# Attention and SwiGLU FFN on one core: loads ordered by need, masks built on chip, four tiles ahead of the FFN, and q and k transposed by DMA

## The chip, the cores and the metric

The kernel runs on one core of one Trainium2 chip. The metric is the device time of one execution in microseconds (us). A profiled execution also gives a span, from the first to the last instruction, which stands about 2 us below the time. A program can also fall into a slower state with a lower granted TensorE clock.

## The reference, cut to what matters

```python
# q, k, v: (8 batches, 8 heads, 576 rows, 64), fp32
rel    = pos[:, None] - pos[None, :]
mask   = (rel >= 0) & (rel < 128)                   # causal window of 128
scores = (q @ k^T) / 8 - slope[h] * |rel|           # ALiBi; -1e9 outside the mask
x      = softmax(scores) @ v                        # -> (4608 tokens, 512)
g      = x @ w_gate                                 # 512 -> 1536
out    = (silu(g) * (x @ w_val)) @ w_out            # 1536 -> 512, fp32
```

## The kernel before

Two batches are taken together and cut into nine tiles of 128 rows; the fifth holds the last 64 rows of both. With four such pairs there are 36 tiles of q, k and v, called ranks here. The attention takes the tiles of a pair in the order of their rows, with the combined one last, and the scores of a tile need its own rank and the next: tile 4 of the attention needs ranks 5 and 6, and tile 9, the first of the second pair, ranks 9 and 10. The attention of a tile is: transpose q and k, scores, exp on ScalarE, product with a mask of ALiBi weights on VectorE, values, division, transpose of x. The FFN takes 512 tokens (four tiles) as a block. Its matmuls are mixed with the attention of later tiles in program order, and TensorE executes in that order.

Transposes of q and k run on TensorE, and VectorE copies them out of PSUM, the memory into which the program's matmuls write:

```python
pt = ps_a.tile([P, 8, P], FP16, name="pt", tag="a")
for j in range(4):
    nc.tensor.transpose(pt[:, j, :], tk[:, 2 * j:2 * j + 2, :], idm)
for j in range(4):
    nc.tensor.transpose(pt[:, 4 + j, :], tq[:, 2 * j:2 * j + 2, :], idm)
nc.vector.tensor_copy(kTs[s][:, :, cols], pt[:, 0:4, :])
nc.vector.tensor_copy(qTs[s][:, :, cols], pt[:, 4:8, :])
```

The attention emits the scores of tile i + 1 ahead of the values of tile i, always. Loads of the inputs and weights go through GpSimd's queue and convert fp32 to fp16 on the way. Their order at the start is:

```python
loads_to(1); load_w(wg2, wg_sb, 0, 128);   load_w(wv2, wv_sb, 0, 128)
loads_to(3); load_w(wg2, wg_sb, 128, 512); load_w(wv2, wv_sb, 128, 512)
loads_to(4); load_mask("lo")
# ... [cut: w_gate and w_val from column 512 on]
loads_to(5)
# ... [cut: w_out, two transfers]
loads_to(7); load_mask("hi"); load_mask("com")
```

The softmax here doesn't subtract the row's maximum and nothing guards it: scores larger than these inputs give would overflow.

## Time and profile before

| | before |
|---|---|
| time, median of 3 runs | 411.18 us (411.11 to 411.3) |
| span of the profiled run | 409.1 us |
| first gate matmul of the FFN | 59.3 us |
| long stage, from there to the last output matmul | 344.9 us, TensorE idle 3.6 |
| tail | 4.9 us |

The kernel is two stages: a start in which TensorE waits for loads, and a long stage in which TensorE is full. The prediction below shows the lines for that. In the profiles PE is TensorE, PEld its loads of weights, DVE VectorE, ACT ScalarE, POOL GpSimd and SP SyncE; L with a number is a line of the kernel. The DMA queues (packets, MB, and the sum of the packets' times as a share of 16 engines' span) and the time from issue to landing (columns: transfer, queue, kind and count, KB each, median us):

```profile
q0 software_dynamic: 118304, 18.88, 62.0%
q1 hardware_dynamic: 5968, 11.31, 8.1%
...
out_dram<-osb SPq DMA_DIRECT2D x32, 256.0 KB, 2.0
kn<-in_k_dram POOLq DMA_DIRECT2D x32, 128.0 KB, 3.7
```

The packet times of the converting loads (q0, 18.88 MB) add up to 62%. Packets overlap (the same kind of sum, the DMA share of the windows below, goes up to 2.43 here), so this tells how much is in flight, not how long the engines are busy. The hardware queue (q1: masks and output stores) has little to do, and an output store is in DRAM 2.0 us after its issue.

### The profile page before, as it was taken

How to read it: one execution, taken by the hardware profiler on the slowest of the kernel's cores; microseconds unless marked ns; L12 is line 12 of the kernel's file. 1: busy time of each engine (PE TensorE's matmuls, PEld its weight loads, DVE VectorE, ACT ScalarE, POOL GpSimd, SP SyncE). 2: the span in 40 equal slices, each digit the busy share in tenths (PEclk: the TensorE clock that was granted, in tenths of full speed). 3: DMA queues.
4: the chain of work that ended last, by engine and by line, in shares of the span. 5: the costliest groups of instructions: out<-in, count | busy, mean ns of one | idle time of the engine just before them, and what ended most of it. 6: DMA issues, size and time to landing. Idle time of an engine off the chain costs nothing.

```text
span 409.1 us, 6645 instructions
## 1 busy us (share of the span) xinstructions
PE 364.4 (89%) x2592; PEld 181.0 (44%) x2592; DVE 245.9 (60%) x500; ACT 173.8 (42%) x317; POOL 112.0 (27%) x170
## 2 busy tenths in 40 slices
PE   0571289999999999999999999999999999999995
PEld 0240134455545445444454454455544445444442
DVE  0351057876587567675885586758865864572550
ACT  1241055534455455445644555455444543323321
POOL 7974485053424211542260104111000000000000
PEclk9999999999999999999999999999999999999998
DMA  9999999269969652799696527654011000101104
GB/s 221 164 192 193 182 155 95 14 42 80 124 66 66 64 79 38 52 82 116 64 68 63 79 38 48 82 79 29 0 53 51 2 27 26 51 2 51 54 12 91
DMA packets 124304, 30.62 MB, mean 75 GB/s; under 512 B 114544, under 2 KB 119152, under 8 KB 124272
## 3 DMA queue, kind: packets, MB, share of 16 engines
q0 software_dynamic: 118304, 18.88, 62.0%
q1 hardware_dynamic: 5968, 11.31, 8.1%
q8 instruction: 20, 0.33, 0.3%
q14 instruction: 12, 0.10, 0.1%
HBM read 39.62 MB, written 9.44 MB: 120 GB/s over the span
## 4 chain that ended last, share of the span: by engine, by line
PE 73%; DMA 10%; DVE 7%; ACT 5%; issue 2%; POOL 1%; DVEq 0%; POOLq 0%; ACTq 0%
PE po L322 22%; PE pv L308 20%; PE pg L295 20%; DMA kn<-in_k_dram 6%; DMA wv_sb<-in_moe_w_val_dram 4%; ACT exr L223 4%; PE ps L209 3%; PE av L254 3%; PE px L281 3%; DVE uu L300 2%; PE pt L162 1%; PE pt L164 1%; DVE hT L310 1%; DVE exl L227 1%; DVE ex L227 1%
## 5 line engine op out<-in xcount | busy, mean ns | idle before, releaser
L308 PE MATMUL pv<-xT,wv_sb 128*128 128x512 f16 x432 | 112.0, 380 | 1.4 <-DVE uu L300 1.2
L295 PE MATMUL pg<-xT,wg_sb 128*128 128x512 f16 x432 | 112.0, 381 | 0.3
L300 DVE SCALAR_TENSOR_TENSOR uu<-tt,pg 128x512 f16<-128x512 f16 x108 | 73.8, 684 | 61.6 <-ACT tt L298 61.2
L322 PE MATMUL po<-wo_sb,hT 128*128 128x512 f16 x432 | 104.8, 379 | 0.9 <-ACT osb L326 0.7
L298 ACT ACTIVATE tt<-pg 128x512 f16<-128x512 f32 x108 | 65.1, 603 | 79.5 <-PE pg L295 77.6
L223 ACT ACTIVATE exr<-ps 128x512 f16<-128x512 f32 x128 | 67.4, 608 | 39.7 <-PE ps L209 39.7
L310 DVE TENSOR_TENSOR hT<-uu,pv 128x512 f16<-128x512 f16 x108 | 74.0, 685 | 8.3 <-PE ps L209 1.0
L143 POOL DMA_DIRECT2D kn<-in_k_dram x40 | 34.0, 853 | 113.3 <-PE pt L164 101.9
L308 PEld LDWEIGHTS <-wv_sb 128*128 128x128 f16 x432 | 40.8, 98 | 47.4 <-issue 4.4
L322 PEld LDWEIGHTS <-hT 128*128 128x128 f16 x432 | 40.0, 98 | 43.7 <-issue 3.9
L295 PEld LDWEIGHTS <-wg_sb 128*128 128x128 f16 x432 | 39.9, 98 | 43.8 <-issue 3.2
L227 DVE TENSOR_TENSOR ex<-exr,m_reg 128x1024 f16<-128x1024 f16 x48 | 33.1, 689 | 36.2 <-ACT exr L223 36.2
L326 ACT ACTIVATE osb<-po 128x512 f32<-128x512 f32 x36 | 21.6, 600 | 59.0 <-PE po L322 58.9
L282 ACT COPY xT<-px 128x512 f16<-128x512 f16 x36 | 21.0, 584 | 50.9 <-PE px L281 50.8
L162 PE MATMUL pt<-idm,kn 128*128 128x128 f16 x144 | 15.7, 238 | 27.9 <-DMA kn<-in_k_dram 27.0
L143 POOL DMA_DIRECT2D va<-in_v_dram x40 | 33.8, 851 | 7.3 <-POOL va L140 5.0
L143 POOL DMA_DIRECT2D qn<-in_q_dram x40 | 34.1, 854 | 5.1 <-DMA wo_sb<-in_moe_w_out_dram 2.9
L165 DVE COPY kT<-pt 128x512 f16<-128x512 f16 x36 | 15.1, 418 | 31.6 <-PE pt L164 31.4
L257 DVE TENSOR_TENSOR x<-av,rec 128x256 f16<-128x256 f32 x72 | 29.0, 419 | 0.7
L209 PE MATMUL ps<-qT,kT 64*128 64x256 f16 (+1 forms) x288 | 27.2, 282 | 2.3 <-DVE qT L166 2.3
L162 PEld LDWEIGHTS <-kn 128*128 128x128 f16 x144 | 11.1, 105 | 35.4 <-DMA kn<-in_k_dram 29.1
L281 PE MATMUL px<-idm,x 128*128 128x128 f16 x144 | 18.8, 230 | 5.5 <-DVE x L257 5.4
(27 smaller groups left out, 173.5 us busy)
## 6 DMA issues: line engine op xcount, KB each, us to landing
out_dram<-osb SPq DMA_DIRECT2D x32, 256.0 KB, 2.0
kn<-in_k_dram POOLq DMA_DIRECT2D x32, 128.0 KB, 3.7
qn<-in_q_dram POOLq DMA_DIRECT2D x32, 128.0 KB, 5.0
va<-in_v_dram POOLq DMA_DIRECT2D x32, 128.0 KB, 5.3
wo_sb<-in_moe_w_out_dram POOLq DMA_DIRECT2D x2, 768.0 KB, 16.4
wg_sb<-in_moe_w_gate_dram POOLq DMA_DIRECT2D x2, 512.0 KB, 8.7
wv_sb<-in_moe_w_val_dram POOLq DMA_DIRECT2D x2, 512.0 KB, 10.1
out_dram<-osb SPq DMA_DIRECT2D x8, 128.0 KB, 2.3
```

The lines of the kernel that those rows point to most:

```text
L143: nc.gpsimd.dma_start(t_[p0:p1, :, 0:D], src[b, :, r0:r0 + p1 - p0, :].rearrange("h p d -> p h d"))
L162: nc.tensor.transpose(pt[:, j, :], tk[:, 2 * j:2 * j + 2, :], idm)
L209: nc.tensor.matmul(two[par][:, j, o:o + w], kT[rows, pair, kcols], qT[rows, pair, cols], start=(j == 0 and n == 0), stop=(j == 1 and n == ...
L223: nc.scalar.activation(er[:, o:o + 2, :], banks[q4][par], AF.Exp, scale=scale)
L227: nc.vector.tensor_mul(e[:, o, :], er[:, o, :], m[:, o, :])
L281: nc.tensor.transpose(pt[:, kb, :], x[:, kb * P:(kb + 1) * P], idm)
L295: nc.tensor.matmul(pg, wg_sb[:, kb, ms], xT[n][:, kb, :], start=(kb == 0), stop=(kb == NKB - 1))
L298: nc.scalar.activation(tt, pg, AF.Tanh, scale=0.5)
L300: nc.vector.scalar_tensor_tensor(out=uu, in0=tt, scalar=1.0, in1=pg, op0=ALU.add, op1=ALU.mult)
L308: nc.tensor.matmul(pv, wv_sb[:, kb, ms], xT[n][:, kb, :], start=(kb == 0), stop=(kb == NKB - 1))
L310: nc.vector.tensor_mul(hT[n][:, m, :], uu, pv)
L322: nc.tensor.matmul(po, hT[n][:, m, j * P:(j + 1) * P], wo_sb[:, m, :], start=(m == 0), stop=(m == NMB - 1))
```

## The change

It has four intents: (1) load only one of the four masks and build the others from it on VectorE; (2) order the loads at the start by need; (3) let the FFN begin after four tiles, with the scores of tile 4 no longer ahead of the values of tile 3; (4) from rank 9 on, transpose q and k by DMA on SP's queue, which takes 216 transposes from TensorE and 54 copies from VectorE. The diff, cut to its core:

```diff
-QK_BY_DMA = False
+QK_DMA_FROM = 9
...
-    for name, m in (("reg", reg), ("lo", lo), ("hi", hi), ("com", com)):   # 4 masks, each loaded
+    nc.sync.dma_start(reg, reg_d.ap())                                     # 1 mask load
+    def make_lo():
+        nc.vector.memset(lo[:, :, 192:256], 0.0)
+        nc.vector.tensor_copy(lo[:, :, 0:192], reg[:, :, 0:192])
...                                                    [make_hi, make_com alike]
-        if QK_BY_DMA:
+        if rank >= QK_DMA_FROM:
+            for t_, dst in ((natk.pop(rank), kTs[s]), (natq.pop(rank), qTs[s])):
                 nc.sync.dma_start_transpose(
                     dst[:, :, cols], t_.rearrange("p h d -> p (h d)"))
...
-            if i < last:
+            if i < last and i != FIRST - 1:            # FIRST = 4
                 transposes_to(need_rank[i + 1])
                 after = scores(i + 1)
...
-            loads_to(i + 8)
+            if i >= FIRST:
+                loads_to(i + 7)
+                ahead(i)                               # DMA transposes, up to 4 tiles ahead
...
+            if i == FIRST - 1:
+                transposes_to(need_rank[i + 1])
+                for fs in scores(i + 1):
+                    ...
-    loads_to(1) ... loads_to(7)                        [the old order, above]
+    load_qk(0, "kq")
+    for r in range(4):
+        load_qk(r + 1, "q"); load_v(r); load_qk(r + 1, "k")
+    load_w(0, 128); load_w(128, 512)
+    load(5); load_v(4); load_w(512, 1024)
+    load(6); load_w(1024, 1536); load(7); load(8)
+    [then w_out]
...
-        target = base + step * (4.55 * 8) / per_block
+            blk, target = 0, base + 2 * max(0, step - 8)                    # block 0
+            target = base + 32 + (step - 24) * RATE * 8 / 36                # RATE = 5.2
```

Beside these: the tile of v has its column of ones written once instead of for every rank, the intermediate of the FFN lies in 18 column tiles instead of two whole blocks, and the combined tile has another order of slots. The transposes that stay on TensorE take one PSUM slot for q and one for k, and stand right before the scores that need them, no longer a tile ahead.

## The prediction

> **What bounds the kernel now.** I read the engine row and the 40 slices of the page first. TensorE is the busiest engine, but its row is full only from the seventh slice on:
>
> ```profile
> PE 364.4 (89%) x2592; PEld 181.0 (44%) x2592; DVE 245.9 (60%) x500; ACT 173.8 (42%) x317; POOL 112.0 (27%) x170
> ...
> PE   0571289999999999999999999999999999999995
> ...
> DMA  9999999269969652799696527654011000101104
> ```
>
> A slice is 10.2 us, so there are two stages. Up to about 59 us TensorE mostly waits while the DMA engines are full. After that TensorE is full and the DMA engines have room. The table of windows puts the cut where the first gate matmul starts (59.3) and where the last output matmul ends (404.2):
>
> ```profile
> 50.00:59.30 9.30, 7.44 (x65) 4.12 (x64) 4.48 (x14) 3.73 (x8) 9.12 (x19) 1.00 2.43 155
> 59.30:404.20 344.90, 341.27 (x2409) 167.93 (x2408) 229.97 (x458) 158.93 (x290) 69.38 (x100) 1.00 0.53 56
> 404.20:409.10 4.90, 0.00 (x0) 0.00 (x0) 0.00 (x0) 0.60 (x1) 0.00 (x0) 0.75 0.32 71
> ```
>
> The first number is the length, then the busy time of PE, PEld, DVE, ACT and POOL, the clock, the DMA share and GB/s. In the long stage TensorE idles for only 344.9 - 341.3 = 3.6 us: there only less TensorE work makes the kernel shorter. VectorE has 115 us free there. The tail is 4.9 us.
>
> The timeline of the first 60 us says what the first stage waits for:
>
> ```profile
> 9.35 0.61 PE L162 MATMUL pt<-idm,kn 128*128 128x128 f16 x4 [9.35 <-DMA kn<-in_k_dram]
> ...
> 14.54 1.04 PE L209 MATMUL ps<-qT,kT 64*128 64x256 f16 x8 [0.84 <-DVE qT L166]
> ...
> 38.89 0.61 PE L162 MATMUL pt<-idm,kn 128*128 128x128 f16 x4 [7.86 <-DMA kn<-in_k_dram]
> ...
> 49.03 0.61 PE L162 MATMUL pt<-idm,kn 128*128 128x128 f16 x4 [8.69 <-DMA kn<-in_k_dram]
> ```
>
> Three long waits, all for k tiles: the first tile (9.35), and ranks 5 and 6 (38.89, 49.03). A rank is one of the 36 tiles of 128 rows of q, k and v. Rank 6 is needed because the program emits the scores of tile 4 ahead of the values of tile 3, and the FFN needs tiles 0 to 3. In the issue order ranks 5 and 6 stand behind all of w_gate and w_val, and rank 6 behind w_out too.
>
> **What the Trainium skill says.** (1) "DMA: Bandwidth & Descriptors", section "Issuing engines are not separate DMA queues": transfers of all issuers run on the same 16 engines and interleave. The trace agrees: in the first 10 us the SP queue moved 1.87 MB (four masks, identity) and the GpSimd queue 0.35 MB; in the next 10, alone, the latter moved 1.62. (2) The same page, section "SWDGE vs HWDGE vs iDMA": casts go through GpSimd, transposes through SP or ACT. So the fp32 loads must stay on GpSimd, and the new transposes share SP with the output stores. (3) "VectorE: DVE Perf Modes", section "The three transpose paths": a 128x128 16-bit transpose is 390 ns on TensorE and 1309 ns through the DMA crossbar. The trace has 238 ns for one on TensorE, far less in a stream (below); no run here shows a DMA transpose yet. (4) "Advanced Engine Details and Errata", section "X-Bar Transpose (TRN2)", expects 350-400 GB/s for such DMAs. Sections (3) and (4) disagree about the new operation by an order of magnitude, which sets my range.
>
> **The change part by part.**
>
> *Start: masks.* Three of four masks are no longer loaded: 0.5 + 0.5 + 0.25 MB, 1.3 MB. At the 1.87 + 0.35 MB that moved between about 1.7 and 10 us (some 270 GB/s; the middle of that window ran at 300 to 390) this is about 4 us. The first k tile should land at 9.35 - 4 = 5.3 us. Building the masks takes VectorE eight instructions, estimated at 2 us in all from the 0.69 us of a 128x1024 product; by the instruction order they stand among the first copies, in idle time. GpSimd also loses 36 memsets of 0.165 us, which cost nothing.
>
> *Start: order of loads.* 0.131 MB at 155 GB/s is 0.85 us per tile, and the 0.85 us of GpSimd's own issue agrees. The order is k0 q0 q1 v0 k1 q2 v1 k2 q3 v2 k3 q4 v3 k4. From 5.3 that puts k1 near 8.9, k2 11.5, k3 14.1, k4 16.7. Then the first weight columns (0.26 MB at 200 GB/s) land near 18 and the next ones near 22.
>
> *Start: the chain.* With data there, compute sets the pace. In the old trace scores of tiles 0 to 3 start at 14.54, 19.15, 23.80 and 29.16: about 5.4 us a tile at the end, exp to mask to value to division to transpose, and none of the last ones waits for a DMA. The new k1 lands at 8.9, scores 0 start some 1.4 later (as 13.08 to 14.54 before), scores 1 at 13.1 (PSUM slots come free after the exps), then +4.65 and +5.36: scores 3 at 23.1, against 29.16. Tile 4's scores no longer stand ahead. In the old trace the products of tile 3 end at 33.08; values, division, transposes and copies add about 3.2, so 36.3, minus the 6.05 shift: the first gate matmul near 30.5. That is 29 us earlier than 59.3.
>
> *Long stage: transposes.* Back to back they cost TensorE less than their latency:
>
> ```profile
> 204.67 0.39 PE L162 MATMUL pt<-idm,kn 128*128 128x128 f16 x4
> 204.90 0.39 PE L164 MATMUL pt<-idm,qn 128*128 128x128 f16 x4
> 205.12 0.39 PE L162 MATMUL pt<-idm,kn 128*128 128x128 f16 x4
> 205.34 0.39 PE L164 MATMUL pt<-idm,qn 128*128 128x128 f16 x4
> 205.57 1.03 PE L308 MATMUL pv<-xT,wv_sb 128*128 128x512 f16 x4
> ```
>
> From start to start four take 0.22 us, so a rank (eight) takes 0.44, not 8 x 0.238. Before, 112 of the 144 k transposes fall after 59.3, so 28 ranks. After, only ranks 5 to 8 do. 24 ranks x 0.444 = 10.6 us leave TensorE. Added: the scores of tile 4 (0.6). The stage is 344.9 - 10.6 + 0.6 = 334.9. VectorE loses 54 copies of about 0.416, 22.5 us, from an engine that is not the bound.
>
> *DMA transposes.* 54 of 128 KB. Their loads have slack: GpSimd waited 101.9 us for TensorE to free k tiles. The new rate of 5.2 gives 8/1.156 = 6.9 FFN steps per tile, at 0.863 us plus 1.3 of attention: 7.3 us per tile, for two transposes. Output stores of 256 KB land in 2.0 us on SP's queue; with 2 to 2.5 us per transpose the pair takes about 5 and is hidden.
>
> *Losses.* After step 8 of block 0 attention runs at two steps per FFN step, one tile per 5.2 us, equal to the 5.4 us chain, and VectorE has about as much work there as TensorE (21 us each by count of instructions): I add 2.5 us. Scores 9, the first to need DMA transposes, come at about 62; k and q of ranks 9 and 10 come behind w_out and land from 52 to 56, and four transposes follow: I add 2 us.
>
> *Sum.* 30.5 + 334.9 + 2.5 + 2 + 4.9 = 374.8 of span. The time stands 2.1 above the span (411.2 against 409.1): 377.
>
> The per-column FFN tiles (18 buffers in place of two whole blocks), fewer memsets and the combined tile's changed slots cost the same number of main instructions; I give them nothing.
>
> **The rivals.**
> (a) *The DMA transposes become the pace.* With 4 blocks x 1.309 us one takes 5.2, a pair 10.5, against 7.3 available. From 53 us, 27 x 10.5 ends at 337; then about 3 for the last tiles, two FFN blocks (62), the last projections (10.4) and the tail: about 418, slower than now. TensorE executes in order, so late transposes stop the FFN too, and stores behind them on SP hold ScalarE. For it: the skill's smaller figure, and SP's order, which has up to 18 transposes between stores. Against it: section (4), and 16 engines that should work on the four blocks together.
> (b) *The start is won and given back.* The DMA engines are full to 60 us before; after, they must carry the same minus 1.3 MB. If the FFN begins at 30, block 0 could wait for weight columns or ranks 7 to 10 instead. By my landing times columns 512 on arrive at 31 (needed 37), rank 8 at 43 (needed 46): it fits narrowly. If it fails by 5 to 10 us: 382 to 387.
> (c) *The start is bound by the chain more than I think*, since each transpose group now takes its own PSUM slot (two per rank, of four that turn over): one more us a tile gives about 381.
> (d) *Everything hides*: no added losses, 372.
>
> **Range and chances.** The centre is the sum, 377. (d) and a start at 28 give 368; (b) and (c) together give about 390. Range 366 to 391. "Faster" fails only if (a) holds in nearly full size, since the start alone is worth 29 us: faster 0.92, same 0.04, slower 0.04.
>
> **What would show it.** The first k transposes at 5 to 6 us and the first gate matmul at 28 to 33 show the start. In the long stage: 216 fewer TensorE transposes, 54 fewer VectorE copies, stage length about 335 to 340 with idle below 10 us. (a) would show as TensorE waits for DMA before scores, throughout, and landings over 3.6 us; (b) as DMA waits between 30 and 65 us only. I am wrong if the gate matmul starts after 40, or if scores wait for transposes past the second batch pair.

## More of the kernel before

The outputs leave through three buffers and the queue of SP (SyncE), which does little else:

```python
opool = ctx.enter_context(tc.tile_pool(name="op", bufs=3))
# ...
osb = opool.tile([P, DM], FP32, name="osb", tag="osb")
nc.scalar.mul(osb, po, 0.5)                      # ScalarE, from PSUM
for p0, p1, r0 in rows_of(n, j):
    nc.sync.dma_start(out[r0:r0 + p1 - p0, :], osb[p0:p1, :])
```

## The result, and the profile after

| | before | after |
|---|---|---|
| time, median of 4 runs each | 411.14 us | 388.99 us (388.19 to 389.99) |
| span of the profiled run | 409.1 | 386.4 |
| first gate matmul | 59.3 | 29.8 |
| long stage | 344.9 | 351.8 |
| tail | 4.9 | 4.9 |

The long stage is counted to 4.9 us before the end in every run below; in the changed kernel the last matmul ends 0.4 us after that.

The ratio of the times is 0.9466, with a 95% interval of 0.9435 to 0.9497. A ratio here is the mean time of one kernel's fast runs over that of the other's of the same rounds, so it isn't quite the ratio of the medians. The result is correct. The kernel is faster, by 22 us where 34 were predicted, and the 388.99 lies near the upper end of the range.

First the engine row, the slices and the queues of the page after:

```profile
PE 356.6 (92%) x2376; PEld 169.8 (44%) x2376; DVE 232.8 (60%) x461; ACT 173.3 (45%) x317; POOL 108.8 (28%) x134
...
PE   2889996799999959999999999999999999999995
...
PEclk9999999699999978999999999999999999999999
DMA  9999999999999999999201020110011001002004
...
q0 software_dynamic: 118304, 18.88, 75.4%
q1 hardware_dynamic: 34912, 17.08, 23.3%
```

TensorE has 216 instructions fewer, as intended. Counting slices of 9.7 us from 0, its row is full from slice 3 on, but has two dents: slices 6 and 7 (58 to 77 us) and slice 14 (from 135 us). Under each dent, or just after it, the granted clock falls. The DMA row is new too: it is full through slice 18, up to some 180 us, where it had been loose from 70 us on. The times of the same 118304 load packets now add up to 75.4% instead of 62.0% of a longer span, and the hardware queue has 28944 packets more.

The windows (length, busy time of PE, PEld, DVE, ACT and POOL with the number of instructions, clock, DMA share, GB/s), the last for the whole long stage:

```profile
29.70:60.00 30.30, 29.34 (x204) 13.37 (x204) 23.11 (x47) 15.48 (x30) 18.18 (x22) 1.00 1.90 181
60.00:80.00 20.00, 14.10 (x100) 6.25 (x101) 8.35 (x18) 6.52 (x12) 11.98 (x15) 0.83 2.38 131
...
70.00:75.00 5.00, 4.97 (x17) 1.89 (x18) 1.27 (x2) 2.66 (x5) 4.02 (x6) 0.50 2.45 134
110.00:150.00 40.00, 35.23 (x240) 16.66 (x238) 21.97 (x47) 16.39 (x31) 18.58 (x22) 0.91 2.00 175
29.70:381.50 351.80, 337.79 (x2223) 158.55 (x2223) 215.60 (x410) 161.03 (x296) 83.00 (x100) 0.98 0.93 89
```

TensorE idles for 351.8 - 337.8 = 14.0 us in the long stage, against 3.6 before. Of this, 5.9 lie in 60 to 80 and 4.8 in 110 to 150. The clock is lowered in the same two stretches: from 70 to 75 us it is 0.50. The clock's records in the packed trace put the two stretches at 69.19 to 76.01 and 140.87 to 147.69 us. TensorE is busy there (4.97 of 5 us) at half its rate, so a wait costs more than its idle time.

One reading of the clock column is a trap. The clock's records begin at 35.05 us in this trace and at 61.87 in that of before; earlier, the column prints 1.00 for want of a record. The matmuls themselves tell (four matmuls of 512 columns, then the same further on):

```profile
29.76 1.87 PE L302 MATMUL pg<-xT,wg_sb 128*128 128x512 f16 x4 [0.67 <-DMA va<-in_v_dram]
...
35.81 1.03 PE L302 MATMUL pg<-xT,wg_sb 128*128 128x512 f16 x4
```

Within a group of transposes one follows another after 0.107 us in the start and 0.056 later. By this measure the start ran at half clock throughout, and so did the first 5.3 us of the FFN (2.6 in before). The prediction's own lines show it: four transposes take 0.61 us at 9.35, 38.89 and 49.03, and 0.39 at 204.67.

**Stall A, at 64 to 70 us.** The SP queue issues the first DMA transposes, and the scores of tile 9 wait for one of them (start, duration, engine, line, operation; in brackets the idle time before and what ended it):

```profile
58.41 1.26 SPq L173 DMA_TRANSPOSE kT<-kn  x1
59.71 1.82 SPq L173 DMA_TRANSPOSE qT<-qn  x1
```

```profile
70.03 0.40 PE L221 MATMUL ps<-qT,kT 64*128 64x256 f16 x2 [5.87 <-DMA qT<-qn]
```

The second of these landed at 69.90, 10.2 us after its issue. The first four took 8.4, 9.5, 9.8 and 10.2 us. Over the whole run the median was this:

```profile
kT<-kn SPq DMA_TRANSPOSE x27, 7.1
qT<-qn SPq DMA_TRANSPOSE x27, 7.3
```

**Stall B, at 132 to 143 us.** The output copies on ScalarE, then SP's queue in the same stretch:

```profile
118.99 0.60 ACT L330 ACTIVATE osb<-po 128x512 f32<-128x512 f32 x1 [1.97 <-PE po L326]
...
124.18 0.60 ACT L330 ACTIVATE osb<-po 128x512 f32<-128x512 f32 x1
...
130.59 0.63 ACT L330 ACTIVATE osb<-po 128x512 f32<-128x512 f32 x1
...
140.44 0.60 ACT L330 ACTIVATE osb<-po 128x512 f32<-128x512 f32 x1 [8.74 <-DMA out_dram<-osb]
```

```profile
121.28 0.53 SPq L332 DMA_DIRECT2D out_dram<-osb  x1
121.91 2.16 SPq L173 DMA_TRANSPOSE kT<-kn  x1
124.97 1.29 SPq L173 DMA_TRANSPOSE qT<-qn  x1
...
132.59 1.22 SPq L173 DMA_TRANSPOSE qT<-qn  x1
134.34 7.05 SPq L332 DMA_DIRECT2D out_dram<-osb  x4
```

Copies and stores come in the same order, so they can be paired by counting: the store at 121.28 is that of a copy made at 95.47, and the one at 134.34 is that of the copy at 118.99, ready 14.8 us earlier. The queue had the transposes from 121.91 to 132.59 to issue first, six in all, several of which waited for their own k or q tile. The store landed at 140.34, 6.0 us after its issue, so of the 20.8 us from the end of the copy to the landing 14.8 are the queue and 6.0 the transfer. The fourth copy needs the buffer of the first, as there are three, and so ScalarE stood still for 8.74 us, with the FFN's tanh behind it. TensorE ran out of work 4.64 us before the next value matmul:

```profile
142.79 0.58 PE L312 MATMUL pv<-xT,wv_sb 128*128 128x512 f16 x1 [4.64 <-DVE uu L307]
```

This line names VectorE as the releaser. It is only the last link: VectorE waited for ScalarE, ScalarE for a buffer, the buffer for a store, and the store for SP's queue. Reading a single wait would have stopped one or two links early.

So the time came from the start (59.3 - 29.7 = 29.6 us) and part of it went into the long stage (351.8 - 344.9 = 6.9 us): 22.7 us, which is the whole difference of the spans.

### The profile page after: what moved, and what is told of

The parts are those of the page before. It is cut to its first block, busy times and chain, and to the rows that moved or that the text cites. A ratio compares the mean times of both kernels' runs of the same rounds, so it can differ in the third digit from the quotient of the medians.

```text
span 386.4 us, 6223 instructions
## 1 busy us (share of the span) xinstructions
PE 356.6 (92%) x2376; PEld 169.8 (44%) x2376; DVE 232.8 (60%) x461; ACT 173.3 (45%) x317; POOL 108.8 (28%) x134
## 3 DMA queue, kind: packets, MB, share of 16 engines
q0 software_dynamic: 118304, 18.88, 75.4%
q1 hardware_dynamic: 34912, 17.08, 23.3%
## 4 chain that ended last, share of the span: by engine, by line
PE 60%; DMA 22%; DVE 5%; ACT 5%; POOL 3%; issue 3%; SPq 0%; ACTq 0%; POOLq 0%; DVEq 0%
PE po L326 18%; PE pv L312 18%; PE pg L302 17%; DMA qn<-in_q_dram 10%; DMA va<-in_v_dram 5%; DMA qT<-qn 4%; ACT exr L235 4%; PE ps L221 3%; PE av L266 2%; PE px L291 2%; DVE uu L307 2%; DMA out_dram<-osb 2%; DVE ex L239 1%; POOL qn L149 1%; DMA kn<-in_k_dram 1%
## 5 line engine op out<-in xcount | busy, mean ns | idle before, releaser
L312 PE MATMUL pv<-xT,wv_sb 128*128 128x512 f16 x432 | 116.2, 387 | 5.9 <-DVE uu L307 5.7
L302 PE MATMUL pg<-xT,wg_sb 128*128 128x512 f16 x432 | 115.4, 389 | 0.7 <-DMA va<-in_v_dram 0.7
L326 PE MATMUL po<-wo_sb,hT 128*128 128x512 f16 x432 | 103.3, 380 | 0.0
L302 PEld LDWEIGHTS <-wg_sb 128*128 128x128 f16 x432 | 41.3, 100 | 48.1 <-issue 7.4
L221 PE MATMUL ps<-qT,kT 64*128 64x256 f16 (+1 forms) x288 | 26.0, 277 | 6.4 <-DMA qT<-qn 5.9
L266 PEld LDWEIGHTS <-ex 128*128 128x128 f16 x384 | 19.4, 102 | 8.8 <-issue 2.8
L291 PE MATMUL px<-idm,x 128*128 128x128 f16 x144 | 19.6, 231 | 3.9 <-DVE x L269 3.2
L266 PE MATMUL av<-va,ex 128*128 128x65 f16 x384 | 21.3, 201 | 0.6 <-ACT exr L235 0.6
L221 PEld LDWEIGHTS <-kT 64*128 64x128 f16 x288 | 11.9, 97 | 22.5 <-issue 20.1
## 6 DMA issues: line engine op xcount, KB each, us to landing
wv_sb<-in_moe_w_val_dram POOLq DMA_DIRECT2D x2, 512.0 KB, 11.5
```

The lines of the kernel that those rows point to most:

```text
L221: nc.tensor.matmul(two[par][:, j, o:o + w], kT[rows, pair, kcols], qT[rows, pair, cols], start=(j == 0 and n == 0), stop=(j == 1 and n == ...
L266: nc.tensor.matmul(av[:, j, :], w, val, start=(n == 0), stop=(n == len(todo) - 1))
L302: nc.tensor.matmul(pg, wg_sb[:, kb, ms], xT[n][:, kb, :], start=(kb == 0), stop=(kb == NKB - 1))
L312: nc.tensor.matmul(pv, wv_sb[:, kb, ms], xT[n][:, kb, :], start=(kb == 0), stop=(kb == NKB - 1))
L326: nc.tensor.matmul(po, hT[(n, m)][:, j * P:(j + 1) * P], wo_sb[:, m, :], start=(m == 0), stop=(m == NMB - 1))
```

## The experiments

The theory: the start is worth what was planned, and the TensorE time that DMA transposes save is lost again in stalls A and B. A is the latency of the first transposes while many loads are in flight; B is the store behind transposes on one in-order queue, with three buffers. Rivals: only one of the two matters; or the start itself is worth less than it seems. All kernels gave correct results. Each edit is against the changed kernel. Every kernel was timed against the kernel before on the same chip (medians of 410.5 to 411.0 us there; the rounds used three chips). For e1 and h2, with one slow run each, the time is the median of the three fast runs.

| run | time us | ratio to before (95%) |
|---|---|---|
| the changed kernel | 388.99 | 0.9466 (0.9435 to 0.9497) |
| e1: all transposes on TensorE | 388.32 | 0.9447 (0.9413 to 0.9480) |
| e2: DMA transposes from rank 18 | 392.42 | 0.9560 (0.9535 to 0.9584) |
| e3: six output buffers | 380.46 | 0.9261 (0.9242 to 0.9279) |
| e5: stores on ScalarE's queue | 398.67 | 0.9706 (0.9685 to 0.9727) |
| h1: four masks loaded | 390.63 | 0.9501 (0.9471 to 0.9530) |
| h2: tile 4 ahead again | 399.00 | 0.9713 (0.9686 to 0.9740) |
| h3: old order of loads | 385.25 | 0.9379 (0.9357 to 0.9400) |
| e4: from rank 18, six buffers | 376.94 | 0.9187 (0.9153 to 0.9220) |
| x1: three load buffers, six output buffers | 376.77 | 0.9155 (0.9127 to 0.9183) |
| x2: from rank 13, six buffers | 375.79 | 0.9148 (0.9134 to 0.9161) |
| c1: all on TensorE, six buffers | 388.69 | 0.9466 (0.9444 to 0.9487) |
| h4: old order, six buffers | 378.85 | 0.9233 (0.9207 to 0.9260) |

### e1: all transposes on TensorE

```diff
-QK_DMA_FROM = 9
+QK_DMA_FROM = 99
```

> All q and k transposes on TensorE again, the rest of the change kept. Theory (the DMA transposes bring both stalls of the long stage, 5.9 us before scores 9 with a cold clock after it, and 8.7 us of ScalarE behind an output store): both go, 27 ranks x 0.44 = 12 us of TensorE work come back, the first gate matmul stays near 29.8, and the time is 384 to 388, so no slower than the changed kernel's 389. Rival (the stalls come from the full DMA engines and stay without the transposes): 12 us are added to the same stalls, 398 to 402. Second rival (the DMA transposes are worth their 10.6 us in full): also near 400.

The three fast runs took 386.69 to 389.2 us, as long as the changed kernel. The 54 DMA transposes, in place of 216 on TensorE, are therefore worth nothing in the change as it stands. The profiled execution of this kernel fell into a slow state not seen in any other run, 626.77 us at a mean clock of 0.58:

```profile
PEclk9965555555555555555555555555555555555555
```

It is left out of the comparison, its cause is open, and it is why the control c1 was made below.

### e2: DMA transposes from the third pair on

```diff
-QK_DMA_FROM = 9
+QK_DMA_FROM = 18
```

> DMA transposes start with the third batch pair (rank 18), ranks 9 to 17 go through TensorE. Theory (scores 9 wait because the transposes of ranks 9 and 10 share full DMA engines with the loads): the 5.9 us wait before scores 9 goes and its cold clock with it, about 8 us, 9 x 0.44 = 4 us come back, and the wait of ScalarE for a store stays: 384 to 386. Rival (that wait is the landing of the loads of ranks 9 and 10 themselves): the wait stays as a wait of the TensorE transposes for a load at about 60 us, 391 to 394.

It took 392.42 us: more than expected, and more than the changed kernel. The window shows that stall A went, and the waits (total, times, longest) that stall B grew:

```profile
60.00:80.00 20.00, 19.97 (x173) 10.57 (x174) 13.69 (x30) 10.63 (x20) 15.57 (x20) 1.00 2.89 131
```

```profile
ACT osb L330 <- DMA out_dram<-osb: 16.2, 2, 11.2
```

The longest wait of ScalarE for a store, 11.2 us, ended at 182.07, and TensorE stood still for 8.86 us until 183.21, with the clock halved after it. The nine ranks given back to TensorE cost time too (about 5 us by the 0.57 a rank that c1 gives below). The miss taught that the two stalls aren't independent parts of a sum: removing one moved the schedule into a larger case of the other. To size A, B had to be gone first.

### e3: six output buffers

```diff
-    opool = ctx.enter_context(tc.tile_pool(name="op", bufs=3))
+    opool = ctx.enter_context(tc.tile_pool(name="op", bufs=6))
```

> Six output buffers in place of three. Theory (a store held behind transposes on the SP queue keeps a buffer, and ScalarE, and then TensorE, wait 8.7 us for it near 132): the wait of ScalarE for an output store goes, TensorE gains its 4.6 us there and the cold clock after it, 1 to 2 us, so 382 to 384. Rival (something else on the DMA queues would have stopped TensorE there anyway, such as transposes for scores): the time stays at 387 to 389 with a new wait near 140.

It took 380.46 us, 8.5 less, a little more than expected. Stores are as late as ever: four left together at 136.83, behind six transposes. But nobody waits for them now, while stall A stays:

```profile
110.00:150.00 40.00, 39.72 (x299) 19.31 (x298) 28.01 (x59) 20.87 (x39) 20.43 (x24) 1.00 2.10 170
```

```profile
PE ps L221 <- DMA qT<-qn: 5.3, 1, 5.3
```

B is thus a matter of buffers, and it cost 8.5 us of time, of which only 4.64 are in TensorE's wait. The halved clock from 142.79 to 147.69 us is worth about 2.4 more (an estimate: half of that stretch). The remaining 1.5 was not divided.

### e5: stores on another queue

```diff
-                    nc.sync.dma_start(out[r0:r0 + p1 - p0, :], osb[p0:p1, :])
+                    nc.scalar.dma_start(out[r0:r0 + p1 - p0, :], osb[p0:p1, :])
```

> Output stores issued from ScalarE's queue, three buffers as in the changed kernel. Theory (the order on SP holds the stores, not the transfer itself): stores go out at once, land in 6 to 8 us while the DMA engines are full, and the wait of 8.7 us falls to 0 to 2: 382 to 385. Rival (the full DMA engines make the store slow wherever it is issued): a wait of 3 us or more for a store stays, 386 to 389. ScalarE pays some 0.5 us per issue, which it has free.

This should have freed the stores from the transposes. It took 398.67 us, outside what either theory expected, and 10 us worse than the changed kernel. The waits say where:

```profile
ACT xT L292 <- DMA qT<-qn: 13.2, 1, 13.2
...
PE ps L221 <- ACT xT L292: 12.9, 2, 9.3
```

ScalarE itself waits for a DMA transpose, though none of its work reads one. The trace shows how: the DMAs of both queues use eight semaphores in turn, and the issue of a store waits for the one that it is given. The store issued at 96.79 us had the semaphore of a transpose that was issued at 89.4 and landed at 96.7. So the coupling didn't go; it moved from SP, where waiting cost nothing by itself, onto ScalarE. The cause is read from the waits and was not tested by a further run.

### h1, h2, h3: the parts of the start

h1 loads the three other masks at the beginning again and does not build them:

```diff
+    [full_masks() makes the three masks on the host's side of the build, as constants]
+    for name, t_, m in zip(("lo", "hi", "com"), (lo, hi, com), full_masks()):
+        nc.sync.dma_start(t_, nc.inline_tensor(m, name="mask_" + name).ap())
-            if i == 1:
-                make_lo()
-            if i == 5:
-                make_hi()
-                make_com()
```

> The three further masks are loaded at the start again (1.3 MB), nothing built on the chip. Theory (they share the DMA engines with the first tiles and delay every load behind them by about 4 us): first k tile at 9.3 instead of 5.8, first gate matmul at 33 to 34, and since the wait before scores 9 hangs on the same loads, the whole time rises by about 4: 392 to 394. Rival (the start is bound by the chain of compute, not by loads): gate below 32 and a time of 389 to 390.

The first transpose came at 9.73 us (5.76 in the changed kernel) and the first gate matmul at 33.40, so 3.6 later. Kernels that share the beginning of the changed one start the FFN at 29.76 to 31.4 us, so 3.6 is more than their spread. The time is 1.6 us longer, and the intervals overlap: inconclusive for the time, clear for the start.

h2 puts the scores of tile 4 ahead of the values of tile 3 again:

```diff
-            if i < last and i != FIRST - 1:
+            if i < last:
...
-            if i == FIRST - 1:
-                transposes_to(need_rank[i + 1])
-                for fs in scores(i + 1): ...
```

> Scores of tile 4 stand ahead of the values of tile 3 again, so the FFN waits for rank 6, which lands near 36. Theory A (the DMA engines, full to 70 us, set when scores 9 can run, so a start before about 36 is given back there): gate near 41, 11 us later, but the wait of 5.9 us before scores 9 and the cold clock behind it vanish, and scores of tile 4 are already done: 389 to 393. Theory B (the earlier FFN counts in full, the wait before scores 9 is tied to SP's queue and stays): 398 to 401.

The three fast runs took 398.12 to 399.91 us, 10.0 more by the medians. Its profiled run fell into the slow state (407.18 us, clock 0.94), so its lengths are only rough: the first gate matmul came at 45.40, 15.6 later, the wait at tile 9 was gone, and a single wait for a store had 11.8 us. A later start thus costs less than its length here, because it spares stall A.

h3 restores the old order of loads:

```diff
-    load_qk(0, "kq")
-    for r in range(4): load_qk(r + 1, "q"); load_v(r); load_qk(r + 1, "k")
+    load(0); load(1)
     load_w(0, 128)
+    load(2); load(3)
     load_w(128, 512)
-    load(5); load_v(4)
+    load(4)
     load_w(512, 1024)
-    load(6)
     load_w(1024, 1536)
+    load(5); [w_out]; load(6)
     load(7); load(8)
-    [w_out]
```

> The loads in the old order (weights between ranks, ranks 5 and 6 behind the weights), masks built on the chip, four tiles ahead of the FFN. Ranks 0 to 4 are then in by about 22.5 (17.6 in the changed kernel), so the gate starts near 31 to 32, and scores of tile 4 wait for rank 6 until about 46. Theory (what makes the early start is that tile 4 is no longer ahead; the order itself is worth 2 us at the gate): 389 to 393, gate at 31 to 33. Rival (the order of loads is the main part of the gain): gate after 38 and 396 or more.

It took 385.25 us: 3.7 less than the changed kernel, with the first gate matmul 1.1 later, at 30.90. The 1.1 lies within the spread named under h1. So the new order of loads brought nothing to this kernel. In its trace a q tile comes 4.5 us late at 46 us, and a wait of kind B is there (ScalarE 9.7 us for a store, TensorE 6.1 us at 96), but nothing waits at tile 9:

```profile
60.00:80.00 20.00, 19.98 (x171) 9.70 (x169) 15.81 (x35) 11.53 (x22) 13.04 (x17) 1.00 2.45 143
```

### e4: both stalls removed

```diff
-QK_DMA_FROM = 9
+QK_DMA_FROM = 18
-    opool = ctx.enter_context(tc.tile_pool(name="op", bufs=3))
+    opool = ctx.enter_context(tc.tile_pool(name="op", bufs=6))
```

> DMA transposes from rank 18 on and six output buffers: both stalls should be gone. Theory (the two stalls are separate: one is the transposes of ranks 9 and 10 among full DMA engines, the other a store held on SP's queue): no wait over 2 us of TensorE after 30 us, 380.5 - 8 + 4 = 376 to 378. Rival (transposes of the third pair, which follow each other on SP as fast as before, bring their own waits for scores): 379 to 383.

It took 376.94 us, as expected, and has neither stall (TensorE busy for 19.69 of 20 us in 60 to 80, and 39.56 of 40 in 110 to 150). Against e2 the six buffers alone bring 15.5 us.

### x1, x2: why the first transposes are slow

Is A the price of a transpose, or of a transpose behind full DMA engines? x1 has six output buffers and one buffer fewer for q and for k, so that fewer loads run ahead of the transposes:

```diff
-    nat = ctx.enter_context(tc.tile_pool(name="nat", bufs=4))
+    nat = ctx.enter_context(tc.tile_pool(name="nat", bufs=3))
-    opool = ctx.enter_context(tc.tile_pool(name="op", bufs=3))
+    opool = ctx.enter_context(tc.tile_pool(name="op", bufs=6))
```

> Six output buffers as before in this series (380.5 us), and three buffers in place of four for the loaded q and k tiles, so that the loads of rank 12 can't be on the way while the transposes of ranks 9 and 10 are. Theory (the first transposes take 8 to 10 us from issue to landing because they share full DMA engines with loads queued ahead of need): they land in under 8 us, the wait before scores 9 falls from 5.3 to 2 to 4, and the time to 376 to 379. Rival (a transpose takes that long by itself, or by its queue on SP): the wait stays at 5 or more and the time at 380 to 382; three buffers may also make later loads late, over 382.

It took 376.77 us, 3.7 less than e3. The first four transposes landed in 7.6, 8.6, 7.6 and 6.8 us (8.1, 9.3, 9.3 and 9.9 in e3), and the wait shrank:

```profile
PE ps L221 <- DMA qT<-qn: 2.2, 1, 2.2
```

So fewer buffers made it faster, as a theory of crowding says and a fixed price for a transpose doesn't. In e4 single ones landed in as little as 2.4 us. A is mostly the crowd's doing.

The other traces settle who makes the crowd. c1 (below) and e3 differ only in where q and k are transposed: loads of k land after a median of 4.2 us in c1 and of 9.1 in e3. The output stores, which nobody changed, tell the same: in the changed kernel the eight issued from 89 to 141 us took 5.7 to 7.8 us to land, in c1 those from 73 to 132 us took 2.0 to 4.5, and late in both kernels most take 2.0. So the transposes suffer from the crowd and make much of it themselves. (x1's FFN also began 1.2 us earlier than e3's, at 30.15 against 31.33. Kernels with the same beginning differ that much here, so I don't give all of the 3.7 to A.)

x2 starts DMA transposes at rank 13, which leaves the first transposes four ranks more time:

```diff
-QK_DMA_FROM = 9
+QK_DMA_FROM = 13
-    opool = ctx.enter_context(tc.tile_pool(name="op", bufs=3))
+    opool = ctx.enter_context(tc.tile_pool(name="op", bufs=6))
```

> Six output buffers, DMA transposes from rank 13 on: ranks 9 to 12 through TensorE while the DMA engines are full, the other 23 ranks by DMA. Theory (only the first ranks of the second pair are late; the variant from rank 18 pays 5 x 0.44 = 2.2 us for nothing): no wait for a transpose, 376.9 - 2.2 = 374 to 376. Rival (any transposes begun before about 100 us are late because the DMA engines are full until then): a wait before scores 12 or 13 of 2 us or more and 377 to 380.

It took 375.79 us, the fastest of all, 13.2 less than the changed kernel. TensorE waits for no DMA transpose, and the clock was 1.00. Within this one trace the landing follows the crowd: the first three transposes, issued from 76 to 79.5 us with four loads in flight or fewer (DMA share 0.80 from 76 to 82), took 3.6, 2.5 and 2.5 us; those from 84 to 100 us, mostly with four or five loads in flight (DMA share 2.07), took 5.4 to 8.0. The long stage:

```profile
29.76:368.70 338.94, 333.16 (x2255) 158.60 (x2255) 218.11 (x418) 161.11 (x295) 83.76 (x100) 1.00 0.97 90
```

### c1, h4: two controls

c1 asks whether six buffers would have helped without any DMA transpose:

```diff
-QK_DMA_FROM = 9
+QK_DMA_FROM = 99
-    opool = ctx.enter_context(tc.tile_pool(name="op", bufs=3))
+    opool = ctx.enter_context(tc.tile_pool(name="op", bufs=6))
```

> All transposes on TensorE and six output buffers: the clean reference for what the DMA transposes are worth, and an undisturbed profile of the variant whose profile fell into a state of half clock. Theory (stores waited only because transposes stood before them on SP's queue, so without transposes the number of output buffers is of no account): 387 to 389, as with three buffers, no wait over 2 us of TensorE after the first gate matmul, and the variant with DMA transposes from rank 13 (375.8) is 11 to 13 us below it, near 23 x 0.44 = 10.2. Rival (output buffers limit in any case): 383 or less.

They would not: 388.69 us, like e1. It also gives the fast profile that e1 lacked:

```profile
0.00:30.16 30.16, 18.48 (x152) 11.22 (x153) 17.24 (x51) 11.69 (x21) 24.80 (x35) 1.00 1.74 148
30.16:382.10 351.94, 346.86 (x2440) 169.60 (x2439) 232.94 (x464) 161.90 (x296) 83.80 (x100) 1.00 0.69 70
```

Two things are read from it. Its long stage, 351.94 with no stall, is as long as that of the changed kernel, 351.80: what DMA transposes saved and what their stalls cost are equal. And against x2, whose long stage is 338.94, the 23 ranks that x2 transposes by DMA are worth 13.0 us when nothing stalls, 0.57 a rank.

h4 repeats h3 with six output buffers, to see whether h3's gain was the order itself:

```diff
-    [new order of loads]
+    [old order, as in h3]
-    opool = ctx.enter_context(tc.tile_pool(name="op", bufs=3))
+    opool = ctx.enter_context(tc.tile_pool(name="op", bufs=6))
```

> Loads in the old order and six output buffers, DMA transposes from rank 9. With three buffers this order gave 385.3, with a wait of 6.1 us near 96 that hangs on an output store, and one of 4.5 us for q of rank 6. Theory (the store wait goes, the rank 6 wait stays and takes the place of the wait before scores 9): 376 to 379, below the 380.5 of the changed order, so the order of the loads is no gain as the change has it. Rival (the order helps once the store wait is gone): 381 or more.

It took 378.85 us against 380.46 of e3, with intervals that overlap. With B gone, the two orders can't be told apart by time: each has one long wait near the start of the FFN, the old one at a q tile (3.8 us at 46 us), the new one at tile 9 (5.3 us).

## Why the prediction was right or wrong

**The direction and the start: right.** The first k transpose came at 5.76 us (predicted 5.3), k1 to k4 landed at 9.45, 12.26, 15.04 and 17.64 (8.9, 11.5, 14.1, 16.7), and the first gate matmul came at 29.76 (30.5). What was credited to the parts is another matter. The runs that undo one part give 15.6 us of start for tile 4 no longer ahead, 3.6 for the masks and 1.1, within the spread, for the order. These make 20 of 29.6; the rest appears only when parts act together and was not divided further.

**TensorE's work in the long stage: nearly right in sum.** The transposes saved were sized at 0.444 us a rank, from their spacing in one calm passage. That spacing holds: in c1 one transpose starts 0.056 us after the other, 0.45 a rank. c1 against x2 gives 0.57. Counted from each TensorE instruction's start to the next one's, most of the difference lies in the score matmuls (19.8 us in c1, 17.0 in x2); why is not tested. The work that moves from the start into the full stage was counted at 1.9 us. The start of c1 holds 33 TensorE instructions fewer than that of before (152 against 185), 16 of them transposes and 16 score matmuls, so this is about right too. (The busy times of the two starts, 18.5 and 23.1 us, overstate it, because the start runs at half clock.) Still c1's stage is 7.0 us longer than before's, 1.4 of it idle; beyond the moved work this was not foreseen, and it is not divided. Taking the 27 ranks at 0.57 from c1's 351.9 gives 351.9 - 15.4 = 336.5 for the changed kernel without stalls. That is an estimate from these two runs; the prediction had 334.9.

**The losses: the term that failed.** They were 2.5 (block 0) and 2 (scores 9), 4.5 together. Block 0 came out near its 2.5, by luck: TensorE was idle for only 1.0 of the first 30.3 us, but the first 5.3 of these ran at half clock, a loss of about 2.7 (an estimate) against 1.3 in before, which the prediction had not seen. But the stage ran to 351.8, so 351.8 - 336.5, about 15 us, were lost. The cause of the error is the sentence "with 2 to 2.5 us per transpose the pair takes about 5 and is hidden". That duration was carried over from output stores of before, which ran with few transfers in flight (a DMA share of 0.53 in its long stage). The median was 7.1 to 7.3 us and the first ones took up to 10.2; in the same crowd the stores themselves took 5.7 to 7.8. So what failed was the assumption of a free DMA, not the likeness of a transpose to a store. And stall B, a store that waits behind transposes until three buffers are used up, was not in the sum at all.

The runs divide the 15: e3's stage is 342.7, so 9.1 went with B (some 1.5 of them, by the first clock records at 35.05 and 33.75 us, to the longer stretch of half clock at the beginning); what remains above 336.5, about 6, is A. A second count agrees roughly: idle time beyond x2's, 14.0 - 5.8 = 8.2, and half of the busy time at the halved clock after the two waits, (6.0 + 4.9) / 2 = 5.4, make 13.6. The wait at scores 9 had been foreseen, at the right place and with the right cause, but at a third of its cost; the halved clock after it was not counted at all. The range had been set by two figures of the skill, 1309 ns and 350-400 GB/s, read as a contradiction. They needn't be one: the first is the time of one small transfer, the second a rate. Neither speaks of the crowd, which decided.

**Rival (a) was the right kind, and was dismissed as a whole.** Its last clause, that stores behind transposes on SP hold ScalarE, is stall B word for word. I had tied that to the case of 418 us, in which the transposes set the pace throughout. They did not: scores waited for a transpose only once, and 27 pairs of 10.5 us did not come about. But a queue need not be the pace to do harm. It need only be late by more than three buffers can bear, once. Rival (a) should have been split in two, the small half with a chance of its own.

**Rivals (b), (c) and (d).** (b) named nearly the right amount, 382 to 387 for 389, for the wrong reason: no wait for weight columns of any size appears. Its other candidate, ranks 7 to 10, has a share in A: q of rank 10 landed at 59.2 us, where 52 to 56 was predicted, and the scores wanted it transposed at 64.2 (70.03 - 5.87). (c) did not happen: the gate matmul came 0.7 us earlier than predicted. (d), 372, is within 4 us of x2, the fastest version without stalls.

**The signs.** Idle time in the long stage was to be below 10 us and was 14.0; the stage was to be 335 to 340 and was 351.8; landings over 3.6 us were named as the sign of (a), and they came. The sign "scores wait for transposes past the second batch pair" stayed away. So the signs pointed correctly to a partial (a).

**What stays open.** Why e1 ran once at half clock. How h3 comes to be 3.7 us faster with three buffers: its trace lacks stall A, but has waits of its own, and I have not accounted for the difference. Why the scores take TensorE longer when the transposes run on it, which makes a rank cost 0.57 us rather than the 0.444 of its spacing.

**The better version.** DMA transposes from rank 13 on and six output buffers: 375.79 us, 0.9148 of the time before. Of the 13.2 us that it gains on the changed kernel, 8.5 come from the buffers alone (e3), the rest, 4.7, with the later first transpose.

## What to carry to other kernels

Moving work from a busy engine to a DMA queue also moves it in front of what that queue already carries: count how many new transfers stand ahead of each old one, by how much each can be late, and whether the old one has buffers for it. Size a new transfer by what the DMA engines carry at that moment, itself included, not by another transfer's latency on a quiet stretch, and let it start where fewer loads are in flight. When two stalls lie on one path, remove both before judging either: removing A alone (e2) made the kernel slower here. And check a clock of 1.00 against the spacing of like matmuls before believing it.

## What the Trainium skill lacked or had wrong

- "VectorE: DVE Perf Modes", section "The three transpose paths": its 1309 ns for a 128x128 transpose by DMA does not say how four of them in one instruction behave. Here SP could issue such an instruction (128x512) every 1.3 us, and it landed after a median of 7.1 to 7.3 us, 10.2 at the slowest of the first four, and in 2.4 at best (e4). Neither 1.3 nor 4 x 1.309 = 5.2 us tells what one waits for.
- "Advanced Engine Details and Errata", section "X-Bar Transpose (TRN2)": it expects 350 to 400 GB/s. 128 KB in 2.4 us is 55 GB/s at best here, but that is one transfer's latency, so the rate is not tested. What the transposes cost others is not said: they brought 29376 packets to the hardware queue (34912 in e3, 5536 in c1), and with them alone changed the loads of k took a median of 9.1 us from issue to landing (e3) instead of 4.2 (c1).
- "DMA: Bandwidth & Descriptors", section "Issuing engines are not separate DMA queues": it is borne out (the transposes on SP slow GpSimd's loads, as above), but has no word on order within one issuer. Here a store stood ready for 14.8 us behind six transposes on SP (stall B, 8.5 us by e3). Putting stores on another issuer was worse (398.67 us), with ScalarE waiting up to 13.2 us for a transpose. I found no page that warns of such waits of an issuer.
- "TensorE: Matmul & The Clock Gate", section "What's actually happening": it says that the clock falls to half after an idle window of about 3.4 us. The traces agree in part. After 5.87 us of idle time the clock was 0.50 from 70 to 75 us, and the start ran at half clock, as the section's default says. But waits of 2.24 us (x1, at 65.0) and 1.83 us (h1, at 44.6) were also followed by 3.4 us at 0.50, while waits of 2.10 (x2) and 2.22 us (c1) at 42.5 were not. An execution that stays at 0.56 from 34.9 us to its end, with TensorE busy for 584.7 of 586.1 us (e1, 626.77 us), fits nothing that this section says.
- The same page has a general caveat on the trace's clock events, but not that their records can begin late: here at 61.87 us in before and 35.05 in the changed kernel, though four matmuls of 512 columns took 1.87 us at 29.76 and 1.03 at 35.81.
